# An attention-and-gate kernel on one core: small matmuls as 32-column tiles, frequency rows in 4.5 blocks of 128, and two batches woven step by step

## The chip, the cores and the metric

The kernel runs on one core of a Trainium2 chip. TensorE (PE in the profile) multiplies matrices from SBUF into PSUM, VectorE (DVE) and ScalarE (ACT) do the elementwise work and empty PSUM, GpSimd (POOL) and SyncE (SP) mostly start DMAs. The metric is the time of one execution on the device in microseconds (us), as the median of several runs. "Granted clock" is TensorE's clock as the trace records it, where 1.00 is full speed; "half clock" is a stretch recorded at 0.50.

## The reference, cut to what matters

```python
# attention: B = 8 batches, H = 8 heads, S = 576 positions, D = 64; 32 landmarks
q_lm, k_lm = means of 18 neighbouring rows of q and k       # 32 rows each
A  = softmax(q @ k_lm.T / 8)          # 576 x 32
Bm = softmax(q_lm @ k_lm.T / 8)       # 32 x 32
C  = softmax(q_lm @ k.T / 8)          # 32 x 576
Z  = Bm.T / (norm1(Bm) * norminf(Bm) + 1e-6)
for _ in range(6): Z = 2 * Z - Z @ Bm @ Z                   # Newton
x = A @ Z @ C @ v                     # heads side by side: 576 x 512
# gate
x1, x2, x3 = split(x @ w_proj)        # three times 576 x 512
y = x1 * irfft(rfft(x2) * rfft(filter)) * x3                # along the 576 positions
out = y @ w_out
```

Both kernels do the Fourier transforms as matmuls with tables of sines and cosines. Neither forms x: the gate keeps A (576 x 32 per head) and Z C v (32 x 64 per head) apart, projects the second (tile G), transforms the first (tile Ah), and multiplies the two. A "gate" below is this second part for one batch, an "attention" the first part up to A and Z C v.

## The kernel before

The shapes that matter are these. Eight heads of 32 landmarks are two groups of four heads, so that a group fills 128 rows. The kernel before makes full 128 x 128 matmuls of a group's four 32 x 32 blocks by putting them on the diagonal of a zero matrix. The 288 frequency rows of the half transforms are three blocks of 96.

```python
def load(b):
    ...                                   # k, q, v of one batch by DMA, then:
    for src, dst in ((kn, kT), (qn, qT)):
        nc.sync.dma_start_transpose(dst[:, 0:3 * H, :], src...)
load(0)
...                                       # w_proj, filter, load(1), w_out

# in attention(b): pooling of q, for every head two 128-wide, then two 64-wide matmuls
for h in range(H):
    for x in (0, 2):
        nc.tensor.matmul(pl2[:, 1, h, :], qn[:, h, 2 * x:2 * x + 2, :]..., poolq[:, x // 2, :], ...)
    for par in range(2):
        nc.tensor.matmul(pl2[64 * par:64 * par + 64, 1, h, :], qn[:, h, 2 + par, :], poolq[:, par, :], ...)

def newton(RZ, last):                     # RZ: per group a 128 x 128 block-diagonal R, and Z
    for g in range(2):
        nc.tensor.matmul(pn2[:, g, lo:160], RZ[:, g, 0:128], RZ[:, g, lo:160], ...)
    nc.scalar.copy(nx[:, :, 0:128], pn2[:, :, 0:128])
    nc.vector.tensor_tensor(nx[:, :, 128:160], RZ[:, :, 128:160], pn2[:, :, 128:160], op=ALU.add)

for g in range(2):                        # C times v, all four heads against all four v; diagonal kept
    for c in range(NC):
        nc.tensor.matmul(pv[:, g, 0:320], eC[:, c, 128 * g:128 * g + 128], vn[:, g, :, c, :], ...)

# in gate(b): inverse transform, 3 blocks x cos/sin x 2 halves for each of 4 column blocks j
for f in range(NF):
    for t in range(2):
        for e in range(2):
            nc.tensor.matmul(pi[:, e, 0:HS], Y[:, f, t, P * j:P * j + P],
                             INV[:, f, t, HS * e:HS * e + HS], ...)

att = {0: attention(0)}
tables_fwd(); tables_inv(); filter_spectrum()
for b in range(B):
    if b + 2 < B: load(b + 2)
    if b + 1 < B: att[b + 1] = attention(b + 1)
    gate(b, *att.pop(b))
```

PSUM is divided into two wide tiles of two banks (`ps_w`), two of one bank for the attention alone (`ps_s`) and two of one bank for the rest (`ps_t`). When the kernel is built, the instructions of each engine are put into a fixed order; the order of the program is a priority in this, not the final order, so both kernels have instructions of two batches mixed to some degree.

The softmax here doesn't subtract the row's maximum and nothing guards it: scores larger than these inputs give would overflow.

## Time and profile before

The median is 355.25 us (355.16 to 356.17, 3 runs). The profiled run spans 359.0 us. It is a long one, 360.68 us at a mean granted clock of 0.918; so the stretches below are together some 5 us longer than in the median run. I divide it by the start of the first matmul of each gate's forward transform, which the trace shows at 95.1, 130.2, 164.6, 199.1, 233.7, 266.5, 300.8 and 325.8 us:

| Stretch | us | What it holds |
|---|---|---|
| front | 95.1 | attention 0 and 1, tables, filter |
| six woven periods | 205.7, on average 34.3 | a gate with the attention of a later batch |
| the last two gates | 58.2 | gates 6 and 7 alone |

From the page of the kernel before, the busy times, and the busy tenths of PE, VectorE and the granted clock in 40 slices of 9 us:

```profile
PE 273.6 (76%) x2728; PEld 167.9 (47%) x2744; DVE 196.1 (55%) x431; ACT 149.4 (42%) x247; POOL 35.8 (10%) x74
...
PE   0300146375999989989999999899989989889793
...
DVE  1020127894667477645963695468467735652651
...
PEclk9999997556599999998998999899999995899999
```

PE is busy for about a fifth of the first eight slices and for 90% of most from the eleventh on. The chain of work that ended last (start us, us, what) tells what the front waits for:

```profile
5.07 6.05 DMA kn<-in_k_dram
11.14 7.35 SPq L122
18.55 30.76 DMA qT<-qn
51.22 3.21 PE w L263 x12
...
65.30 1.65 DVE t L353 x2
```

L122 is the transpose by DMA. The transposed queries of batch 0 land 31 us after their issue, and the sine tables (L353) begin only after that, at 65 us. The list of waits (engine, line, what it waited for: us in total, times, longest) has the same on PE:

```profile
PE w L175 <- DMA kT<-kn: 17.9, 1, 17.9
...
PE w L175 <- DMA qT<-qn: 9.9, 1, 9.9
```

The busy times by stretch, one woven period and the two last gates (stretch, us; busy us and instructions of PE, PEld, DVE, ACT, POOL; granted clock, DMA share, GB/s):

```profile
127.50:162.00 34.50, 32.13 (x345) 20.38 (x346) 23.58 (x49) 17.48 (x30) 3.78 (x5) 0.97 0.84 126
...
299.00:325.00 26.00, 22.66 (x143) 13.16 (x142) 15.49 (x26) 9.87 (x13) 0.00 (x0) 0.85 0.00 1
325.00:359.00 34.00, 25.23 (x147) 13.54 (x146) 12.93 (x17) 13.86 (x20) 0.00 (x0) 0.99 0.25 70
```

A period is PE-bound: PE is busy 32.1 of 34.5 us, VectorE and ScalarE far less. Two details of PE's timeline matter later (start us, us, engine, line, operation, tiles, shapes, count):

```profile
160.17 2.31 PE L263 MATMUL w<-vb_114,eC 96*128 96x320 bf16 x8
...
170.66 0.21 PE L158 MATMUL s<-poolq,qn 96*64 96x32 bf16 x2
170.80 0.21 PE L152 MATMUL s<-poolq,qn 96*128 96x32 bf16 x2
170.94 0.21 PE L158 MATMUL s<-poolq,qn 96*64 96x32 bf16 x2
```

The C-times-v matmuls of 320 columns start 267 ns apart here, about half speed. Each pair of q-pooling matmuls takes 140 ns, 70 ns per matmul, while the k pooling, all of one shape, takes 25 ns per matmul.

### The profile page before, as it was taken

To read this page: it belongs to the slowest core of one execution; us is meant where nothing else is said; L and a number is where in the kernel's file an instruction comes from. 1 tells how busy PE (TensorE), PEld (TensorE's weight loads), DVE (VectorE), ACT (ScalarE), POOL (GpSimd) and SP (SyncE) were. 2 spreads that over 40 slices of the span, in tenths; PEclk is the share of its full clock that TensorE was granted. 3 is DMA by queue.
4 is the path that set the end of the run, shared out by engine and by line. 5 is a ranking of instruction groups with operands and counts; after the bars stand their busy time and mean duration, and the time that the engine had idled before them with its cause. 6 is when DMAs were issued, how large, how long until landed. Compare 5 with 4: busy or idle time off the path is not lost.

```text
span 359.0 us, 6643 instructions
## 1 busy us (share of the span) xinstructions
PE 273.6 (76%) x2728; PEld 167.9 (47%) x2744; DVE 196.1 (55%) x431; ACT 149.4 (42%) x247; POOL 35.8 (10%) x74
## 2 busy tenths in 40 slices
PE   0300146375999989989999999899989989889793
PEld 0300135133466556655664566466556654364361
DVE  1020127894667477645963695468467735652651
ACT  1000121438362565175426733572366263625512
POOL 9520010020101011001100110100000000000000
PEclk9999997556599999998998999899999995899999
DMA  2999999993919399459918991990130040003004
GB/s 30 192 196 165 168 188 165 173 133 29 171 18 129 103 169 144 49 150 147 150 19 187 155 123 29 177 130 0 31 105 0 2 131 2 2 0 112 22 0 132
DMA packets 69518, 36.14 MB, mean 101 GB/s; under 512 B 51376, under 2 KB 64176, under 8 KB 69488
## 3 DMA queue, kind: packets, MB, share of 16 engines
q0 software_dynamic: 26352, 16.84, 35.8%
q1 hardware_dynamic: 43136, 18.88, 29.9%
q8 instruction: 21, 0.34, 0.4%
q14 instruction: 9, 0.07, 0.1%
HBM read 33.69 MB, written 9.44 MB: 120 GB/s over the span
## 4 chain that ended last, share of the span: by engine, by line
PE 51%; DVE 18%; ACT 12%; DMA 10%; issue 4%; SPq 2%; POOL 1%; DVEq 0%; ACTq 0%; POOLq 0%
PE w L486 9%; PE po L498 9%; DMA qT<-qn 9%; PE w L263 6%; DVE T L461 6%; PE w L474 6%; PE w L444 4%; PE w L432 4%; DVE y L490 3%; PE w L455 3%; DVE gt L481 3%; ACT G L437 3%; ACT os L504 2%; PE w L409 2%; SPq L122 2%
## 5 line engine op out<-in xcount | busy, mean ns | idle before, releaser
L486 PE MATMUL w<-INV,Y 96*128 96x288 f16 x384 | 54.8, 286 | 0.2
L474 PE MATMUL w<-AT,G 128*128 128x288 f16 x256 | 41.8, 285 | 6.5 <-DVE gt L481 3.6
L486 PEld LDWEIGHTS <-Y 96*128 96x128 bf16 x384 | 35.9, 97 | 12.9 <-DVE Y L463 2.9
L498 PE MATMUL po<-wout,y 128*128 128x512 bf16 (+1 forms) x144 | 38.9, 380 | 3.4 <-DVE cm L213 1.4
L461 DVE TENSOR_TENSOR T<-X,HH 96x2048 bf16<-96x2048 bf16 x24 | 28.6, 1217 | 23.6 <-ACT X L459 23.6
L474 PEld LDWEIGHTS <-G 128*128 128x128 bf16 x256 | 24.1, 97 | 20.5 <-issue 12.3
L437 ACT CAST G<-w 128x1024 bf16<-128x1024 f32 x24 | 23.5, 1014 | 24.2 <-PE w L432 24.2
L490 DVE TENSOR_TENSOR y<-w,gt 128x576 bf16<-128x576 f32 x32 | 24.2, 756 | 14.6 <-PE w L486 14.6
L504 ACT COPY os<-po 128x512 f32<-128x512 f32 (+1 forms) x32 | 18.7, 584 | 26.7 <-PE s L208 18.5
L238 DVE TENSOR_TENSOR RZ<-RZ,s 128x64 f16<-128x64 f16 x48 | 10.4, 217 | 33.3 <-ACT RZ L237 32.4
L459 ACT CAST X<-w 96x1024 bf16<-96x1024 f32 x24 | 23.4, 1007 | 5.2 <-PE w L455 3.9
L175 PE MATMUL w<-lm,kT 64*128 64x32 bf16 x384 | 9.2, 176 | 21.4 <-DMA kT<-kn 17.9
L455 PE MATMUL w<-G,Ah 128*96 128x512 bf16 x96 | 23.8, 378 | 1.4 <-ACT G L437 1.0
L498 PEld LDWEIGHTS <-y 128*128 128x128 bf16 (+1 forms) x160 | 14.7, 99 | 15.7 <-issue 4.1
L248 ACT ACTIVATE eC<-w 96x512 bf16<-96x512 f32 x24 | 13.4, 594 | 19.0 <-PE w L175 19.0
L444 PE MATMUL w<-F,AE 96*128 96x288 f16 x96 | 16.6, 324 | 5.2 <-ACT G L437 5.2
L237 ACT CAST RZ<-s 128x256 f16<-128x256 f32 x40 | 15.0, 374 | 13.2 <-PE s L232 12.4
L175 PE MATMUL w<-lm,qT 64*128 64x32 bf16 x384 | 10.0, 177 | 12.7 <-DMA qT<-qn 9.9
L175 PEld LDWEIGHTS <-kT 64*128 64x128 bf16 x384 | 6.8, 94 | 26.5 <-DMA kT<-kn 18.1
L232 PE MATMUL s<-RZ 128*128 128x160 f16 (+1 forms) x96 | 15.5, 246 | 4.7 <-DVE RZ L238 2.9
L432 PE MATMUL w<-wproj,ZC 128*64 128x512 bf16 x96 | 18.1, 451 | 0.2 <-ACT Ah L447 0.2
L257 ACT ACTIVATE eA<-w 96x512 bf16<-96x512 f32 x24 | 13.8, 609 | 9.7 <-PE w L175 9.7
(204 smaller groups left out, 414.5 us busy)
## 6 DMA issues: line engine op xcount, KB each, us to landing
kn<-in_k_dram POOLq DMA_DIRECT2D x8, 576.0 KB, 7.0
qn<-in_q_dram POOLq DMA_DIRECT2D x8, 576.0 KB, 6.7
out_dram<-os SPq DMA_DIRECT2D x24, 192.0 KB, 2.5
out_dram<-os SPq DMA_DIRECT2D x24, 128.0 KB, 2.4
vb_112<-in_v_dram POOLq DMA_DIRECT2D x8, 288.0 KB, 9.4
vb_114<-in_v_dram POOLq DMA_DIRECT2D x8, 288.0 KB, 8.0
wproj<-in_moe_w_proj_dram POOLq DMA_DIRECT2D x1, 1536.0 KB, 21.5
out_dram<-os SPq DMA_DIRECT2D x24, 64.0 KB, 2.0
```

Source lines behind the costliest of these rows:

```text
L175: nc.tensor.matmul(dst[:, o // 64, h * m:(h + 1) * m], T[o:o + 64, lo:lo + P], lm[o:o + 64, t, h, :], start=True, stop=True, skip_group_ch ...
L432: nc.tensor.matmul(pg[64 * pp:64 * pp + 64, g, :], ZC[:, 2 * g + pp, :, :].rearrange("p h l -> p (h l)"), wproj[:, 2 * g + pp, Dm * jb:Dm ...
L437: nc.scalar.copy(G[:, :, Dm * jb:Dm * (jb + 1)], pg)
L444: nc.tensor.matmul(pf[:, par, 0:HS], AE[:, par, c, 128 * g:128 * g + 128], F[:, c, :, lo:lo + Q], start=(c == 0), stop=(c == 2))
L455: nc.tensor.matmul(px[:R, t, :], Ah[:, g, t, R * f:R * f + R], G[:, g, Dm:2 * Dm], start=(g == 0), stop=(g == 1))
L459: nc.scalar.copy(X, px[:R])
L461: nc.vector.tensor_tensor(T, X.unsqueeze(2).to_broadcast([R, 2, 2, Dm]), HH[:, f], op=ALU.mult)
L474: nc.tensor.matmul(px[:, e, 0:HS], G[:, g, lo:lo + P], AT[:, g, HS * e:HS * e + HS], start=(g == 0), stop=(g == 1))
L486: nc.tensor.matmul(pi[:, e, 0:HS], Y[:, f, t, P * j:P * j + P], INV[:, f, t, HS * e:HS * e + HS], start=(f == 0 and t == 0), stop=(f == NF ...
L490: nc.vector.tensor_tensor(y[:, j, :].rearrange("p (e s) -> p e s", e=2), pi[:, :, 0:HS], gt, op=ALU.mult)
L498: nc.tensor.matmul(po[:n], y[:, j, i0:i0 + n], wout[:, j, :], start=(j == 0), stop=(j == 3))
L504: nc.scalar.copy(os[:n], po[:n])
```

## The change

Its intent is to give the 32 x 32 problems to PE as 32-column tiles, several of which run side by side in the array, instead of as block-diagonal operands. With that go: the frequency rows in two blocks of 128 and a rest of 32 rows, of which four pieces share one tile ("4.5 blocks"); a third wide PSUM tile in place of the two small extra ones; copies moved from VectorE to ScalarE; batch 0 transposed on PE instead of by DMA; loads issued first; and a program order that takes steps of gate b and attention b+1 in turn. The diff is cut to its core:

```diff
+def _weave(a, b):          # takes the steps of two lists in turn, in proportion to their lengths
-    ps_w ... bufs=2; ps_t ... bufs=2; ps_s ... bufs=2
+    ps_w ... bufs=3;                  ps_s ... bufs=2
+    load(0, by_dma=False)             # first of all; then w_proj, filter; constants after that
@@ newton
-            for g in range(2):
-                nc.tensor.matmul(pn2[:, g, lo:160], RZ[:, g, 0:128], RZ[:, g, lo:160], ...)
-            nc.scalar.copy(nx[:, :, 0:128], pn2[:, :, 0:128])
-            nc.vector.tensor_tensor(nx[:, :, 128:160], RZ[:, :, 128:160], pn2[:, :, 128:160], op=ALU.add)
+            mm(pn[:, 1], identh, RZ[:, 1], start=True, stop=False)
+            for g in range(2):
+                for a in range(4):
+                    o = slice(32 * a, 32 * a + 32)
+                    mm(pn[o, lo:2, g, :], RZ[o, 0, g, :], RZ[o, lo:2, g, :], start=False, stop=True)
+            nc.scalar.copy(nx, pn)
@@ C times v
-                nc.tensor.matmul(pv[:, g, 0:320], eC[:, c, 128 * g:128 * g + 128], vn[:, g, :, c, :], ...)
+                    for a in range(4):
+                        mm(pv[32 * a:32 * a + 32, 128 * g:128 * g + 128],
+                           eC[:, c, 128 * g + 32 * a:128 * g + 32 * a + 32], rhs, ...)   # v of one head, and ones
@@ projection: 4 matmuls of 64 columns by 128 rows -> 8 of 32 columns by 64 rows
@@ inverse transform
-            for f in range(NF): ...                          # 12 matmuls per j
+            for f in range(2): ...                           # 8 matmuls per j
+            o = slice(64 * (j // 2), 64 * (j // 2) + 64)
+            for e in range(2):                               # and 2 with 64 rows
+                mm(pi[:, e, 0:HS], st["YE"][o, ...], INV[o, 4, HS * e:HS * e + HS], ...)
@@ main loop
-    att = {0: attention(0)}
+    attention 0 (its keys and queries transposed by matmuls), load(1), w_out
     tables_fwd()
     tables_inv()
     filter_spectrum()
     for b in range(B):
         if b + 2 < B:
             load(b + 2)
-        if b + 1 < B:
-            att[b + 1] = attention(b + 1)
-        gate(b, *att.pop(b))
+        _weave(gate(b, res.pop(b)), attention(b + 1, ...))
```

## The prediction

> **What bounds the kernel now.** The profiled run takes 359.0 us (355.25 us unprofiled). The chain of work that ended last and the timeline show three stretches.
> (1) A front of 93 us before the first gate matmul. The DMA transposes of batch 0 land late: in the chain, qT is issued at 18.6 us and takes 30.8 us to land. PE waits 17.9 us for kT and 9.9 us for qT (list of waits), so the first attention ends only near 60 us. The sine tables stand behind it in VectorE's order and run at 65 to 85 us, though VectorE idles from 21 to 39 us.
> (2) Six woven periods (attention b+2 with gate b) of 34.5 us. The windows view gives PE 32.1, VectorE about 22, ScalarE 17 us per period, granted clock 0.92 to 0.99: PE-bound.
> (3) Two gates alone, 60 us (299 to 359), latency-bound: PE is busy 48 of them.
>
> **Per period, on PE** (start-to-start times from the timeline: 122 ns at 288 columns, 216 at 512).
> Inverse: 48 to 40 matmuls of 288 columns, -1.0 us. Spectrum: 12 to 8 of 512 columns plus 16 small tiles, -0.3. Output: 20 to 16 of 512 columns plus 8 small, -0.4. Projection from 2.1 to about 1.2 us. C times v, from 12 matmuls of 320 columns to 48 of 128 in four column strips, -0.6. Newton about even. Together -3 us.
> Against it: more changes of tile shape. The Trainium skill ("TensorEngine Tiling (Array Packing)", Key Properties) says that changing the tiling mode drains the engine. The trace agrees: the q pooling, which alternates 128- and 64-wide tiles, takes 70 ns per matmul, the k pooling 25. I estimate 30 more changes at 80 ns, +2.4 us.
> VectorE loses about 4.5 us (Newton adds 6 x 0.22, a third of T and Y about 1.3, the output copy 0.68, masks): 22 to 17.5 us. ScalarE stays near 17.
> So the arithmetic alone saves little. The weave and the third wide PSUM buffer should remove waits: a period holds about 28.5 us of matmul issue at full clock; 6 us are waits and slow-clock stretches (C times v runs at 267 ns, half speed). Expected period 30.5 us.
>
> **Front.** Batch 0 is transposed on PE; loads are issued at 1 us, not 5. First attention ends at about 31 us, tables and filter at 45, instead of 85; gate 0 starts near 46, woven with attention 1. The landing of batch 1 holds up the first period: 34 us.
>
> **Back.** Only one gate runs alone (attention b+1 with gate b, seven periods instead of six): 26 us to the end.
>
> Sum: 46 + 34 + 6 x 30.5 + 26 = 289, plus a little overlooked: 292 us unprofiled. Most of the gain (45 us) is in the front.
>
> **Signs.** Right if: no PE wait on transposes of batch 0; first gate matmul before 55 us; periods of 29 to 32 us; PE busy over 85%; VectorE total near 155 us; one lone gate at the end. The step of the periods is wrong if they stay at 33 us or more with PE issuing little tiles slowly; that of the front, if tables or loads of batch 1 hold gate 0 back past 60 us.
>
> **What would make it wrong.** Drains dearer than 80 ns; loads of 32 columns not overlapping matmuls; woven attention standing in PE's order before its data; VectorE's normalisation chain stalling each period's start.
>
> Chances: faster by over 2% 0.96, within 2% 0.03, slower 0.01. Range 278 to 310 us.

## The result

The changed kernel takes 295.33 us (293.59 to 296.96, 4 runs) against 355.71 us (355.16 to 359.61, 4 runs). The ratio is 0.828, interval 0.821 to 0.836. Ratios here and below are not quite the ratio of the medians. The profiled run spans 291.9 us. The gates begin at 52.7, 84.6, 114.2, 143.7, 174.3, 204.8, 234.4 and 263.9 us:

| Stretch | before, us | after, us | difference |
|---|---|---|---|
| front | 95.1 | 52.7 | -42.4 |
| woven periods | 6, together 205.7 | 7, together 211.2 | +5.5 |
| gates alone | 2, together 58.2 | 1, 27.9 | -30.3 |
| mean of a woven period | 34.3 | 30.2 | -4.1 |

The stretches must be read together. The front before also held attention 1, which is now woven into gate 0; so one more period is woven and one gate fewer stands alone. The page of the changed kernel:

```profile
PE 249.2 (85%) x3642; PEld 149.3 (51%) x3642; DVE 166.6 (57%) x365; ACT 145.9 (50%) x247; POOL 31.9 (11%) x69
...
PE   0776108979999999999999999999989998999990
...
DVE  1279994066834684368417761867186718682830
...
PEclk9999999978999999999979998999999999999998
```

PE is 90% busy in nearly every slice from the tenth to the last but one. A woven period and the last gate:

```profile
83.00:112.60 29.60, 28.79 (x446) 17.40 (x445) 17.53 (x36) 16.83 (x30) 2.52 (x3) 1.00 0.88 143
...
263.00:292.00 29.00, 21.33 (x177) 11.43 (x175) 10.89 (x16) 12.34 (x17) 0.00 (x0) 0.95 0.29 82
```

PE is still the bound of a period, now 28.8 of 29.6 us at full clock, and VectorE fell from 22 us (most periods from gate to gate; 23.6 in the stretch shown) to 17.5 us. From the list of waits and PE's timeline of the changed kernel:

```profile
PE w L77 <- DVE fs L501: 14.5, 1, 14.5
...
PE s L77 <- DMA qn<-in_q_dram: 0.9, 1, 0.9
```

```profile
29.40 1.14 PE L393 MATMUL s<-identh,A 96*128 96x96 f16 x12 [0.44 <-DVE A L363]
45.09 6.59 PE L77 MATMUL w<-fs,F 96*128 96x512 f16 x18 [14.54 <-DVE fs L501]
...
116.29 1.20 PE L77 MATMUL s<-poolq,qn 96*128 96x32 bf16 x16
...
135.07 0.85 PE L77 MATMUL s<-vb_76,eC 96*32 96x128 bf16 x48
```

Attention 0 ends at 32 us on VectorE, and at 30.5 us on PE. Then PE waits 14.5 us, because VectorE makes all tables before it adds the halves of the filter (tile fs). The 48 small C-times-v matmuls take 0.8 us; within each four, which lie in different column strips, the starts are 2 to 5 ns apart, and over all 48 the average is 16 ns. This agrees with the Trainium skill, "TensorE: Matmul & The Clock Gate", Part 3, which gives about 4 ns between matmuls that lie in different tiles of the array. The q pooling takes as long as before, 16 matmuls in 1.2 us.

To see where a period's PE time went, I summed, for each group of matmuls, the time from its start to the start of the next matmul (so waits are counted with the group before them; one period of each trace, from the start of a gate to the next):

| Group | before, us | after, us |
|---|---|---|
| C times v | 2.78 | 0.79 |
| projection | 2.11 | 1.03 |
| scores of A and C (same shapes) | 3.36 | 2.38 |
| inverse transform | 6.42 | 5.52 |
| output | 4.57 | 4.13 |
| Newton | 2.09 | 1.77 |
| spectrum | 2.66 | 2.84 |
| x1 and x3 (same shapes) | 4.44 | 5.18 |
| q pooling (same shapes) | 2.28 | 2.26 |
| all | 34.4 | 29.6 |

Half of Newton's 2.09 us before is not Newton: from its last matmul to the start of the gate there are 1.07 us, most of them a wait. The table alone would say that the small tiles gained most of the 4.8 us, C times v and the projection first. The experiments say something else.

### The profile page after: what moved, and what is told of

Read it like the earlier page. It is cut to its first block, busy times and chain, and to the rows that moved or that the text cites. A ratio compares the mean times of both kernels' runs of the same rounds, so it can differ in the third digit from the quotient of the medians.

```text
span 291.9 us, 8299 instructions
## 1 busy us (share of the span) xinstructions
PE 249.2 (85%) x3642; PEld 149.3 (51%) x3642; DVE 166.6 (57%) x365; ACT 145.9 (50%) x247; POOL 31.9 (11%) x69
## 4 chain that ended last, share of the span: by engine, by line
PE 73%; DVE 11%; ACT 9%; DMA 3%; issue 2%; POOL 0%; ACTq 0%; POOLq 0%
PE w L77 50%; PE s L77 20%; DMA qn<-in_q_dram 3%; DVE T L580 3%; ACT X L578 2%; ACT eC L301 2%; ACT G L569 2%; PE s L190 1%; DVE Y L582 1%; PE s L393 1%; DVE u L408 1%; ACT lmp L211 1%; DVE u L405 1%; DVE t L439 1%; DVE Bn L235 1%
## 5 line engine op out<-in xcount | busy, mean ns | idle before, releaser
L77 PE MATMUL w<-INV,Y 128*128 128x288 f16 x256 | 37.7, 287 | 0.2 <-ACT x_5153 L614 0.2
L77 PE MATMUL w<-wout,y 128*128 128x512 bf16 x128 | 30.2, 380 | 0.0
L77 PEld LDWEIGHTS <-Y 128*128 128x128 bf16 x256 | 22.0, 98 | 8.5 <-DVE Y L582 1.4
L580 DVE TENSOR_TENSOR T<-X,HH 128x2048 bf16<-128x2048 bf16 x16 | 19.5, 1221 | 11.3 <-ACT X L578 11.3
L644 ACT COPY os<-w 128x1024 f32<-128x1024 f32 x16 | 16.2, 1013 | 15.8 <-PE w L77 15.8
L77 PE MATMUL w<-G,Ah 128*128 128x512 bf16 x64 | 20.7, 427 | 3.0 <-ACT eC L301 2.9
L77 PE MATMUL s<-poolq,qn 96*128 96x32 bf16 (+1 forms) x256 | 19.6, 196 | 0.9 <-DMA qn<-in_q_dram 0.9
L77 PE MATMUL w<-fs,F 96*128 96x512 f16 x18 | 6.6, 548 | 14.5 <-DVE fs L501 14.5
L77 PEld LDWEIGHTS <-qn 96*128 96x128 bf16 (+1 forms) x256 | 15.1, 104 | 6.8 <-issue 1.6
L578 ACT CAST X<-w 128x1024 bf16<-128x1024 f32 x16 | 16.4, 1022 | 3.6 <-PE w L77 3.5
L287 ACT CAST RZ<-s 128x128 f16<-128x128 f32 x40 | 10.6, 265 | 12.7 <-PE s L77 12.7
```

Source lines behind the costliest of these rows:

```text
L77: nc.tensor.matmul(out_, lhsT, rhs, start=start, stop=stop, skip_group_check=True)
L287: nc.scalar.copy(nx, pn)
L578: nc.scalar.copy(X, px)
L580: nc.vector.tensor_tensor(T, X.unsqueeze(2).to_broadcast([P, 2, 2, Dm]), HH[:, f], op=ALU.mult)
L644: nc.scalar.copy(os, po)
```

## The experiments

All twelve results agreed with the reference. The changed kernel did not run again in these rounds, and the rounds used several chips, so comparisons with it go over the kernel before, whose median moved between 355.7 and 359.2 us. Against the kernel before, the record calls e1 to e4 faster and leaves e5 to e12 unclear; of these, only e9 has an interval that reaches 1 (0.961 to 1.002). One trace was kept of each run. In each experiment the number in brackets is the mean of the woven periods, from one gate's start to the next, which leaves front and end out. It is 34.3 us before and 30.2 us for the changed kernel.

**Theory.** The periods got shorter because the small tiles cost less PE time, and the weave filled what was left of the waits. The front got shorter because PE no longer waits for the DMA transposes. **Rivals.** The weave or the third wide PSUM tile did it, the small tiles little; in the front, the earlier loads and tables did it.

### e1: without the weave

```diff
-        _weave(gate(b, res.pop(b)), nxt)
+        for s in nxt + gate(b, res.pop(b)):
+            s()
```

> The changed kernel, but each step's program order is the whole attention of batch b+1, then the whole gate of batch b, as before the change; tiles, buffers and front stay. Theory A (the periods became shorter because small tiles issue faster; the scheduler interleaves the two batches anyway, as it did before): within 1%, about 296 us, periods of 29.5 to 30.5 us. Theory B (the weave itself removed the waits of a period): periods go back to 32 us or more, 312 to 325 us.

It took 339.94 us, ratio 0.953 to the kernel before, 45 us slower than the changed kernel (36.9 us for the first six periods; the seventh holds only the end of an attention). Theory A falls; theory B holds for the periods, but the time lies 15 us above its range. PE's timeline shows the beginning of an attention:

```profile
161.86 0.63 PE L77 MATMUL s<-wout,y 128*64 128x256 bf16 x8
162.42 0.77 PE L77 MATMUL s<-poolk,kn 96*128 96x32 bf16 x24
163.04 2.35 PE L77 MATMUL s<-poolq,qn 96*128 96x32 bf16 x32
166.07 0.58 PE L77 MATMUL s<-lmp,dup 128*128 128x512 f16 x1 [0.68 <-ACT lmp L211]
167.44 0.24 PE L77 MATMUL s<-lm 64*32 64x32 bf16 x8 [0.78 <-DVE lm L215]
```

The attention starts only when the gate before it has ended, and its chain of small dependent steps leaves PE waiting 0.4 to 0.8 us at a time. The windows show a second loss:

```profile
162.00:198.40 36.40, 33.19 (x434) 18.70 (x435) 18.61 (x36) 15.95 (x28) 2.51 (x3) 0.72 0.72 115
```

The clock records say half clock (0.50) for 117 us of the span, all such stretches added up, 165.2 to 185.6 us among them, against 18 us in the changed kernel and 61 us in the long run profiled before. In this state the forward transform's matmuls start 240 ns apart instead of 122.

### e9: without the weave, PE kept busy

```diff
+        def warm(t, n):                   # useless matmuls into a tile that is overwritten
+            if not first:
+                for i in range(n):
+                    mm(t, dup..., INV[:, i % 4, 0:512])
             pl3 = stile()
+            warm(pl3, 5)                  # 5 also in the scores of B, 3 in its residual, 1 per Newton step
```

> The kernel without the weave (e1, 340 us, half clock for 117 us of its span), with useless matmuls added on PE where it waited in an attention: 5 of 512 columns before the landmark product, 5 before the scores of B, 3 before its residual, 1 in each Newton step; their results are overwritten. They add some 4 us of PE work per period and save no wait. Theory (most of what the weave gives is that PE never idles long enough for the clock to be halved): half-clock time falls below 50 us and the kernel gets faster in spite of the added work, 310 to 325 us. Rival (the weave gives by the waits it fills): the half clock doesn't matter, 340 us or more.

Half clock fell from 117 to 39 us as expected, but the time was 346.51 us (38.3 us for the first six periods): not faster than e1. So "most of it is the clock" is not shown. One period ran at full clock throughout:

```profile
140.40:175.80 35.40, 34.16 (x464) 19.37 (x463) 18.24 (x36) 16.79 (x30) 2.51 (x3) 1.00 0.76 113
```

The added matmuls took 4.5 us of it (18 of the 19 are in the trace). Taking them off whole would leave 30.9 us, against 36 to 37 in e1; this is an estimate, and a low one, since they stood partly in waits. How the 6.7 us of e1's loss per period divide between waits and half clock stays open; in e1 both begin where an attention stands alone.

### e2: two wide PSUM tiles instead of three

```diff
-    ps_w = ctx.enter_context(tc.tile_pool(name="ps_w", bufs=3, ...))
+    ps_w = ctx.enter_context(tc.tile_pool(name="ps_w", bufs=2, ...))
```

> The changed kernel with two wide PSUM buffers instead of three. Theory A (tiles): under 2%, at most 300 us. Theory B2 (the third wide buffer removed the waits for PSUM): periods up by 1.5 us or more, 306 us or more, with PE waits on ScalarE and VectorE evacuations back in the list of waits.

It took 317.63 us, ratio 0.887, 22 us slower than the changed kernel (33.3 us). Theory A falls; as theory B2 said, waits of PE for the emptying of PSUM are back: 4.4 us in all for X, 3.6 for G and 3.0 for y, against 0.3 us for X and nothing listed for the others in the changed kernel. The third tile alone is not enough: e1 has it too.

```profile
119.70:152.40 32.70, 29.77 (x446) 18.71 (x446) 17.75 (x36) 16.75 (x30) 2.51 (x3) 0.95 0.76 128
```

PE's busy time rose by 1 us per period and its idle time by 2; half clock was 42 us.

### e10: no weave, PSUM divided as before

```diff
-    ps_w ... bufs=3; ps_s ... bufs=2
+    ps_w ... bufs=2; ps_t ... bufs=2; ps_s ... bufs=2     # ps_t: transposes of A, rests of spectrum and output
```

> The kernel without the weave (e1), with the PSUM tiles divided as before the change: two wide ones, two for the attention alone, two for the other small results. So it is the schedule of the kernel before, with small tiles and 4.5 blocks. Theory (without the weave, e1 suffers because the shared small PSUM tiles tie the next attention to the end of the gate, which the kernel before did not): periods of 31 to 33 us, 305 to 322 us. Rival (small tiles bring nothing without the weave): periods of 34 us or more, 325 us or more.

It took 333.39 us, ratio 0.945 (35.2 us). The theory falls and the rival holds. The periods are as long as those of the kernel before, though all the small tiles and the 4.5 blocks are there:

```profile
138.70:173.60 34.90, 33.79 (x452) 19.62 (x444) 18.42 (x37) 16.78 (x29) 2.51 (x3) 0.84 0.83 123
```

The granted clock is 0.84, with half clock for 95 us of the span. So what the small tiles saved on PE did not shorten a period; slow clock and waits took its place. Its gain over the kernel before lies outside the periods (first gate at 66.5 us instead of 95.1).

### e5, e6, e7: one part of the tiling undone, weave kept

```diff
@@ e5: C times v
-   48 matmuls of 128 columns in four column strips
+   12 matmuls of 320 columns; the diagonal picked out by 8 small VectorE instructions
@@ e6: Newton and its first residual
-   8 tiles of 32 x 32 a step and one matmul with the identity
+   2 matmuls of 160 columns with block-diagonal operands a step, and the addition on VectorE
@@ e7: frequency rows
-   two blocks of 128 and a rest
+   three blocks of 96 (tables, filter, spectrum and inverse as before the change)
```

> The changed kernel with only C times v back to 12 matmuls of 320 columns per batch (all four heads of a group in one 128-wide tile, the diagonal picked out by VectorE). At full clock 12 matmuls of about 135 ns are 1.6 us on PE against 0.79 us for the 48 small ones in the changed kernel's trace. Theory (small tiles save PE time in a PE-bound period): +0.8 us per batch, 300 to 304 us. Rival (most of the fall from 2.9 us before was the half clock that hit these matmuls there, and the rest hides): under 3 us slower.

> The changed kernel with only the Newton iteration back to 128-wide block-diagonal operands (2 matmuls of 160 columns a step, and an addition on VectorE). PE time of these groups was 1.8 us per batch with small tiles and should be 1.0 to 1.3 us with wide ones; each step's chain gets about 0.35 us longer. Theory (woven, the chain is hidden): within 1% of the changed kernel, 293 to 298 us. Rival (the chain sets the pace): 302 us or more.

> The changed kernel with the frequency rows back in three blocks of 96 (48 instead of 40 matmuls in the inverse transform, 12 of 512 columns instead of 8 and 16 small ones in the spectrum; a third round of T and Y on VectorE). Theory (PE-bound period): +1.0 to 1.4 us per batch, 303 to 307 us. Rival (the two half blocks and their tile changes cost what they save): within 3 us of the changed kernel.

e5 took 303.05 us, ratio 0.856 (30.9 us; 30.7 in the periods at full clock against 29.6). C times v took 1.63 us of PE per period against 0.79, as expected: at full clock the small tiles are worth 0.8 us of PE here (1.1 us by the periods), not the 2.0 us of the table above. The rest of that fall was the half clock in the kernel before, whose own matmuls start 135 ns apart where the clock is full. e6 took 294.69 us, ratio 0.830 (30.1 us): small-tile Newton brings nothing measurable; it needs more PE time than the wide form (1.77 us of PE for the six steps against 0.94 and 0.06), and less of VectorE. Here PE had 0.8 us less to do, and 14 changes of tile shape fewer (see e8), and a period at full clock became only 0.2 us shorter (29.4 us): saving PE time alone does not always shorten a period. e7 took 308.85 us, ratio 0.870, more than expected; but 12 us of its loss is in its front (first gate at 64.6 instead of 52.7 us, as the build put attention 1 ahead of the filter). Its periods are 30.6 us when undisturbed, 1.0 us longer, as expected.

### e12: all three undone, weave kept

The diffs of e5, e6 and e7 together.

> The changed kernel, weave and three wide PSUM buffers kept, with three parts of the change undone at once: C times v (e5), Newton (e6) and the blocks of 96 (e7). Alone they lengthened a period of 29.6 us by 1.1, 0 and 1.0 us. The front of e7 was 12 us longer by its order of instructions, so the periods are to be compared, not the totals. Theory (weave and small tiles add, the weave being the larger): periods of 31.5 to 32.5 us, some 317 to 328 us in all. Rival (the small tiles are what makes the weave work, as e10 says that tiles without weave bring nothing): periods of 34 us or more, as in the kernel before.

It took 314.2 us, ratio 0.880 (31.2 us), just under both ranges of the theory. The rival falls.

```profile
122.00:153.00 31.00, 29.32 (x356) 19.06 (x356) 21.68 (x50) 17.67 (x29) 3.10 (x4) 1.00 0.83 132
```

With the old shapes for these three and the new order, the clock is 1.00 in this stretch and undisturbed periods are 31.3 us. So we have four corners (mean woven period). They are not clean: e12 keeps the small tiles of the projection, the 4.5 blocks of the output and the copies on ScalarE, e10 keeps the new order inside a gate and the copies, and the trace before is of a long run, which may add up to 0.9 us to its 34.3:

| | attention, then gate | woven, three wide PSUM tiles |
|---|---|---|
| wide tiles, blocks of 96 | 34.3 (before) | 31.2 (e12) |
| small tiles, 4.5 blocks | 35.2 (e10) | 30.2 (after); 29.6 at full clock |

The weave with its third PSUM tile brings some 2 to 3 us per period with the wide tiles (3.1 by the table) and 5.0 with the small ones. The small tiles bring 1.0 us with the weave (1.7 between periods at full clock; the first period of e12 is short, as part of its attention ran in the front) and nothing without it.

### e3: batch 0 transposed by DMA

```diff
-    load(0, by_dma=False)
+    load(0)
-    a0 = attention(0, res[0], first=True)
+    a0 = attention(0, res[0])
```

> The changed kernel with the keys and queries of batch 0 transposed by DMA as in the kernel before, instead of on PE; loads keep their new early place. Theory C (the front got shorter by the PE transposes): PE waits of 15 us or more for kT and qT return, gate 0 starts near 75 us instead of 52.6, 315 to 322 us. Rival D (it got shorter by the order of the loads and the earlier tables): at most 8 us slower, 296 to 303 us.

It took 314.99 us, ratio 0.884, with the first gate at 72.1 us and the same periods afterwards (30.2 us).

```profile
30.22 0.50 PE L77 MATMUL w<-lm,kT 64*128 64x32 bf16 x24 [14.66 <-DMA kT<-kn]
...
40.89 0.82 PE L77 MATMUL w<-lm,qT 64*128 64x32 bf16 x48 [9.26 <-DMA qT<-qn]
```

The transposes on PE are worth 19.4 us of the front. Theory C holds (its first gate was expected near 75 us), but they are less than half of the 42 us by which the first gate moved. e10 gives a second part: its front is the new one but holds attention 1, as before, and its first gate is at 66.5 us, so moving attention 1 out brought some 14 us. The 9 us left by subtraction are the earlier loads and tables, which no run separates.

### e4: the filter ahead of the inverse tables

```diff
-    tables_fwd(); tables_inv(); filter_spectrum()
+    weights(); tables_fwd(); filter_spectrum(); tables_inv()
```

> The changed kernel with the filter spectrum ahead of the tables of the inverse transform in program order. The 14.5 us in which PE waits for the filter sums on VectorE should shrink, since VectorE made 8 us of inverse tables first: gate 0 starts at 46 us instead of 52.6, 288 to 291 us. Rival (the front is bound by the landing of batch 1, or the inverse tables then delay gate 0): within 2 us of the changed kernel.

It took 288.29 us, ratio 0.807, with the first gate at 45.7 us, as expected. PE's wait for fs was halved:

```profile
37.81 6.85 PE L77 MATMUL w<-fs,F 96*128 96x512 f16 x18 [7.18 <-DVE fs L504]
```

### e8: q pooling grouped by shape

```diff
             for h in range(h0, h0 + 4):
                 for x in (0, 2):
                     mm(pl2[:, 1, h, :], ...)                       # 128-wide
+            for h in range(h0, h0 + 4):
                 for par in range(2):
                     mm(pl2[64 * par:64 * par + 64, 1, h, :], ...)  # 64-wide
```

> The changed kernel with the q pooling of four heads grouped by tile shape: eight 128-wide matmuls, then eight 64-wide, instead of two and two in turn. Theory (a change of tile shape drains PE, 80 to 100 ns each): the 32 matmuls go from 2.26 us to about 1.1 us per batch, 286 to 289 us. Rival (their time is the loading of weights, whatever the order): 295 us.

It took 281.4 us, ratio 0.793: 14 us faster than the changed kernel, more than expected (28.4 us in every period). The 16 matmuls of a half take 0.6 us where they took 1.2:

```profile
110.54 0.60 PE L77 MATMUL s<-poolq,qn 96*128 96x32 bf16 x16
```

Counted from the traces, a period has 59 changes of tile shape on PE in the changed kernel (38 before) and 47 here (rows and columns of successive matmuls, rounded up to 32, 64 or 128). Twelve changes fewer are 1.2 us (2.26 to 1.05 us for the group), so 0.10 us a change. The starts show it directly: 25 ns from one 128-wide matmul to the next (in e8), 106 ns to a 64-wide one, 136 ns from a 64-wide pair back to a 128-wide one. It is not the accumulation that waits: in e8 the first 64-wide matmul still comes after 106 ns, though it adds to a head pooled seven matmuls earlier. The Trainium skill, "TensorEngine Tiling (Array Packing)", Key Properties, says that a change of mode drains the engine; this run agrees and gives the price. The gain is more than eight times 1.2 us: half clock also went from 18 to 7 us, and the three periods of the changed kernel that it had lengthened (31.9, 30.6 and 30.5 us) are at 28.4 too. Why the half clock went is not shown.

### e11: e4 and e8 together

> The changed kernel with the q pooling grouped by shape (e8, -14 us) and the filter spectrum ahead of the inverse tables (e4, -7 us) together. One saves in the periods, the other in the front, so they should add: 272 to 276 us. If they don't add (gate 0 then waits for the landing of batch 1 or for the inverse tables): 278 us or more.

It took 275.74 us (273.77 to 276.65), ratio 0.780, interval 0.772 to 0.789. Both gains add: first gate at 44.7 us, periods of 28.4 us after a first one of 30.9. Its interval lies below that of the changed kernel (0.821 to 0.836), so this version beats both kernels.

## Why the prediction was right

The time was 295.33 us, inside the range of 278 to 310 and 3.3 us above the point. The total is closer than its terms, which is partly luck: the front and the back were put 6.7 and 1.9 us too low, the first period and the six others 2.1 and 3.7 us too high, and 3 us had been added for things overlooked. Point by point:

- Front: predicted to the first gate at 46 us, measured 52.7. The mechanism was right (attention 0 ended at 32 us, predicted 31; no wait for transposes). The missing 7 us are the filter step: PE waited 14.5 us for VectorE, and then the 18 filter matmuls of 512 columns took 6.6 us, because the first twelve started mostly 427 ns apart and only the last five 216. Running the filter before the inverse tables (e4) brought the first gate to 45.7 us.
- First period: predicted 34 us, measured 31.9. The reason given was wrong: the loads of batch 1 did not hold it up. PE waits for no load after the first attention, and in e8, whose loads are the same, the first period takes 28.4 us at full clock, like the others. What lengthened it here goes with the half clock. The changed kernel, then e8:

```profile
52.70:84.60 31.90, 29.93 (x433) 17.96 (x429) 18.06 (x37) 18.78 (x32) 2.52 (x3) 0.89 0.88 130
...
51.60:80.00 28.40, 26.12 (x432) 16.35 (x432) 17.91 (x37) 18.39 (x32) 2.51 (x3) 1.00 1.18 149
```

- The other six periods: predicted 30.5 us, measured 29.9 on average. The sum was right, and so was the reading that the arithmetic alone saves little: small tiles gave 1.0 us per period with the weave, 1.7 at full clock (e12), nothing without (e10).
- Terms inside it: C times v was said to save 0.6 us; at full clock it saves 0.8 (e5), and the trace shows 2.0 because the old one ran at half clock. Newton "about even" held in the time (e6) but not on PE, where the small tiles cost 0.8 us more. Thirty more tile changes at 80 ns were 21; at the 100 ns of e8 that is 2.1 us where 2.4 were estimated, if all changes cost what those of the q pooling do, which no run shows. The price had been read from the q pooling, and the 1.2 us that it cost there could have been saved; the change left it untouched.
- Weave: "should remove waits" was right, but the prediction did not see how much hangs on it. Without it the kernel is 45 us slower (e1), without the third PSUM tile 22 us (e2), and half clock is part of it, which the prediction took as something found, though it changed from 18 to 117 us with the schedule alone (e1).
- Back: predicted 26 us, measured 27.9.
- Signs: PE 85% busy and VectorE 17.5 us a period as predicted; VectorE's total was 167 us, not 155. The front alone holds 33 us of it (36 before); how the prediction came to 155 it does not say.
- "Most of the gain is in the front" is right by the table of stretches (42 of the 67 us between the two traces), but it partly renames work: attention 1 left the front because of the weave, and e3 shows 19.4 us for the transposes themselves. By cause, undoing the weave and its PSUM division costs 38 us (e10) and undoing the transposes on PE 20 us (e3), of 60 us in all; that the two add was not tested.

## What to carry to other kernels

When PE time is cut by packing, look first at whether anything fills the time that becomes free: in these runs small tiles gained nothing until two independent batches were interleaved step by step and a third wide PSUM tile kept both streams supplied. Look for changes of tile shape on PE, some 0.1 us each in the q pooling here, and group matmuls by shape where accumulation allows it; this one reordering was worth 14 us, the three tilings undone in e12 some 7 to 12 by their periods. Then measure: 14 changes fewer in e6 brought 0.2 us a period, the twelve of e8 1.2 us. And price a term of the sum only at the clock it will run at: a group seen at half clock promises a saving that belongs to the schedule.

## What the Trainium skill lacked or had wrong

- "TensorEngine Tiling (Array Packing)", Key Properties, says that changing the tiling mode drains the engine but gives no price. Here it is 0.10 us per change (e8: 12 fewer changes, 2.26 to 1.05 us per batch), four times the 25 ns between two k-pooling matmuls.
- "TensorE: Matmul & The Clock Gate", Part 1, says that start-to-start never drops below about 25 ns however small the matmul. For matmuls in different tiles the traces show starts 2 to 5 ns apart, and 16 ns on average over the 48 C-times-v matmuls, weight loads included (0.79 us). The 4 ns agree with Part 3 of the same page.
- The same page's closing table ties the fall to half clock to idle gaps above some 3 us; it also describes frequent micro-idles, but gives no figure for them. In e1 the clock fell at 165.2 us, by its record, with no PE gap above 0.4 us in the 20 us before; what went just before were 56 matmuls of 32 columns, the last 32 of them 70 ns apart on average. That it is the small activity of such matmuls is argued, not shown; that filling the stretch with 512-column matmuls cut half clock from 117 to 39 us is shown (e9).
- The page warns that clock records are unreliable. Where it could be checked here, they were right: in the changed kernel the first record, at 50.3 us, says full clock, and the filter matmuls start 427 ns apart until 50.2 us and 216 ns apart from 50.4 us on. What misleads is the time before the first record, which the profile page counts as full clock.
